# Forward convolution in a hand-set order, and the down-gradient stores on another DMA queue

## The chip, the cores and the metric

One core of one Trainium2 chip. The metric is the device time of one execution in microseconds, the median of 13 runs: 2044.87 us before (2031.46 to 2072.03).

## What is computed

Forward and backward of a gated block on S = 2048 rows, D = 1024 channels, F = 3584 hidden columns, all in bf16:

```python
x = A_q; xn = layernorm(x)
k_shift = sum(k_pad[:, t:t+S] * shift_k[:, ks-1-t] for t in range(4))   # causal, 4 taps
kv = k_shift * v
y = irfft(rfft(kv, 2S) * rfft(ssm_k, 2S))[:S] + kv * ssm_D              # long convolution per channel
s = xn * y
b = ((xn @ w_up) * (xn @ w_gate)) @ w_down
out = x + s * silu(b)
```

The outputs are `out` and the gradients of nine inputs (q, k, v, the shift and convolution weights, D, and the three matrices), for a given `grad_out`.

## The kernel before

The kernel runs in five stages, each bound to a long stream of matmuls on TensorE; the vector work of the convolutions runs beside them. TensorE, VectorE (DVE), ScalarE (ACT), GpSimd (POOL) and SyncE (SP) each run their own instructions in order. SP, ACT and POOL each start DMAs on a queue of their own: `ld` is SP's (L60), `st` POOL's (L65), `sta` ACT's (L71). The order on an engine is chosen by a scheduler from the order of the program and from dependencies; `tc.issue_after(x)` holds an instruction back until after `x` in that order, and `tc.keep_in_program_order` (under `PIN[0]` for VectorE, L205) pins it to where the program has it.

1. Gate and up (L585; to about 577 us). 28 slabs of 256 columns, each against 16 row blocks. A group is 8 matmuls into one psum tile; ScalarE copies it to `gut` (L587), two buffers; four groups are a unit (`gu_unit`). A unit ends with the product gate x up on VectorE into `hN` (L591), its store to `Hd`, and, five groups later, its turn: 8 transposes on TensorE and a store to `HTd`. The first two slabs run block by block behind the layer norm of each chunk of rows. From slab 2 on `tick` is called after each group and pumps the generator `conv_forward` on: the generator yields a weight for each piece of work, in us of VectorE, and the pump takes pieces until their sum has the share of the total that the count of groups has.
2. Down product and the gate's derivative (L988; 577 to 768 us).
3. Gradient of h, and of w_up and w_gate (L1119 and L1136; to 1395 us).
4. Gradient of w_down (L1244, the down gradient; 1395 to 1633 us). For each of 14 slabs of h: a load of 1 MB on SP, two slabs ahead, into three buffers (`load_h`, L1151); 4 groups of 16 matmuls into one of four `psb` buffers; a copy on ScalarE into `wbs` (four buffers, L1246); and two stores of 256 KB on ACT's queue (L1249). Between the loads SP issues DMA transposes of w_gate and w_up (L1202, 1 MB each) and of the gradient dgu (L1209) for the next stage. `tc.issue_after(h_ld[0].ins)` (L1217) puts them after the slab's load. The backward convolution's last units run beside it on VectorE; POOL loads 1 MB tiles A and B for them and stores their results, and slab 11 drains them (L1224) and frees their memory for more transposes.
5. Gradient of x (L1267; from 1633 us to the end), with the dk part beside it.

The forward convolution handles 128 channels at a time, in eight groups `ds`. The steps of one: for each pair of groups the 4-tap shift on VectorE, two halves of 1024 rows (`shift`, L630), ending in `kv`; the filter's rows turned on TensorE (`h_rows`, L651); for kv and then for the filter a forward transform (`fwd4`, L235): four pieces of 16 matmuls (`psF`), each copied to `SP` by ScalarE, then eight additions on VectorE through `W` into `KX` or `HX`; two additions to turn HX (L677); the product of the two on VectorE (`product`, L317); the inverse's additions into `HX` (`inv_dft`, L351); and at last 32 matmuls `psY` with four copies and a store (`tail`, L684). `staggered` (L466) runs one group's tail 12 us of weight into the next group's main part. VectorE's instructions of this stage aren't pinned.

Of the kernel before, what the change touches and what calls it, by code (L numbers as in the profile page):

```python
# [13 lines left out]
BF16 = mybir.dt.bfloat16  # L14
# [5 lines left out]
def build_kernel(  # L20
# [213 lines left out]

    def fwd4(x, X, wp, psp, first=None):  # L235

        W = wp.tile([P, 2, 2, 4, 256], F32, name="W", tag="W")
        c, d = W[:, 0], W[:, 1]
        for i in range(2):
            SP = wp.tile([P, 2, 2, 512], F32, name="SP", bufs=2)  # L240
            for par in range(2):
                ps = psp.tile([P, 2, 2, 256], F32, name="psF")
                cmm(ps[:, 0], T4[par], x, (i, i + 4), first if i == 0 else None)
                cmm(ps[:, 1], T4[par], x, (i + 2, i + 6))
                nc.scalar.copy(out=SP[:, :, par], in_=ps[:].rearrange("p s k x -> p s (k x)"))  # L245
                yield 0.1
            s, q = [SP[:, j].rearrange("p a (k x) -> p (a k) x", k=2) for j in range(2)]
            tt(c[:, i], s, q, ADD)
            tt(d[:, i], s, q, SUB)
            yield 2.5  # L250
        tt(X[:, 0:4, :], c[:, 0], c[:, 1], ADD)
        tt(X[:, 8:12, :], c[:, 0], c[:, 1], SUB)
        yield 2.5
        d0, d1 = [d[:, i].rearrange("p (a k) x -> p a k x", a=2) for i in range(2)]
        tt(two(X, 4, 2, 9), d0, d1[:, :, ::-1], ADD)
        tt(two(X, 12, 2, -7), d0, d1[:, :, ::-1], SUB)
        yield 2.5
    FWD4_W = 0.4 + 4 * 2.5

# [257 lines left out]
    def layer_norm(b0, n, x4):  # L517
# [44 lines left out]
        return last, root, st(xnn[:, c, r0:r0 + n, :], x4[:, 0:n, :])  # L562

    later = []
    gu_mm = [None]
# [4 lines left out]
    def flush(age=0):  # L570
# [3 lines left out]
        while later and later[0][0] >= age:  # L574
            later.pop(0)[1]()

    def gu_unit(sl, b0, n, w, tick):

        gut = fg.tile([P, 2, 4, SLW], BF16, name="gut")
        hN = fg.tile([P, 4, SLW], BF16, name="hN", bufs=3)  # L580
        for i in range(n):
            q, qi = divmod(b0 + i, 4)
            ps = ps_gu.tile([P, 512], F32, name="psg")
            for dc in range(DC):
                gu_mm[0] = nc.tensor.matmul(ps[:], XNT[q][:, dc, qi * P:(qi + 1) * P],  # L585
                                            w[:, dc].rearrange("p a f -> p (a f)"), start=(dc == 0), stop=(dc == DC - 1))
            nc.scalar.copy(out=gut[:, :, i], in_=ps[:].rearrange("p (a f) -> p a f", a=2))  # L587
            flush(5)
            tick()
        sta(GUd[sl, b0 // 8][:, :, b0 % 8:b0 % 8 + n], gut[:, :, 0:n])  # L590
        tt(hN[:, 0:n], gut[:, 0, 0:n], gut[:, 1, 0:n], MUL)  # L591
        st(Hd[sl][:, b0:b0 + n, :], hN[:, 0:n])

        def turn():
            hT = fg.tile([P, 2, 4, P], BF16, name="hT")
            ps = ps_tr.tile([P, 2, 4, P], BF16, name="tr")
            for a in range(2):
                for i in range(n):
                    nc.tensor.transpose(ps[:, a, i, :], hN[:, i, a * P:(a + 1) * P], ident[:])
            nc.scalar.copy(out=hT[:, :, 0:n], in_=ps[:, :, 0:n])  # L600
            fr, so = sl % 12 * SLW, b0 % 8 * P
            st(HTd[b0 // 8][sl // 12][fr:fr + SLW, so:so + n * P].rearrange("(a f) s -> f a s", f=P),
               hT[:, :, 0:n].rearrange("f a i s -> f a (i s)"))
        defer(turn)

    h_out = []

    def conv_forward():
# [21 lines left out]
        def shift(dp):  # L630
# [3 lines left out]
            for c in range(2):  # L634
                k, v = S_.pop(("kv", dp, c))
                acc = U[7][:, 0:2048].rearrange("p (e r d) -> p e r d", e=2, r=8)
                with tc.issue_after(last.ins):
# [13 lines left out]
        def h_rows(ds):  # L651
            hrow = S_.pop(("h", ds))
            hx = cs.tile([P, NB, P], BF16, name="hx")
            for c in range(2):
# [5 lines left out]
                nc.scalar.activation(hx[:, 8 * c:8 * c + 8, :], ps[:], ACT.Copy, scale=WSC)  # L660
                yield 0.1
            h_out.append(ds)
# [3 lines left out]

        def main(ds):
            if ds % 2 == 0:
                yield from shift(ds // 2)
            kvs = S_["kvt", ds // 2][:, ds % 2]  # L670
            yield from h_rows(ds)
            KX = cx.tile([P, 16, 256], BF16, name="KX")
            yield from fwd4(kvs, KX, cs, ps_cv)
            st(KFd[ds], KX[:])
            HX = cs.tile([P, 16, 256], BF16, name="HX", bufs=2)
            yield from fwd4(S_["hx"], HX, cs, ps_cv, S_.pop(("D", ds))[:])
            turned(HX, 1, 0, 1)  # L677
            yield 1.4
            st(HFd[ds], HX[:])
            yield from product(KX, HX, KX, cs, False, 0)  # L680
            yield from inv_dft(KX, HX, cs)
            S_["G", ds] = HX

        def tail(ds):  # L684
            G = S_.pop(("G", ds))
            yf = cs.tile([P, NB, P], BF16, name="yf")
            for rp in range(4):
                ps = inv_rows(G, ps_y, rp)
                nc.scalar.copy(out=by_res(yf[:], rp), in_=rowps(ps))
                yield 0.1  # L690
            st(YFd[:, :, ds * P:(ds + 1) * P], yf[:])

        load_h(0)
        load_kv(0, 0)
        load_kv(0, 1)
        tl = None
        for ds in range(8):
            yield from staggered(main(ds), tl, 12.0)
            tl = tail(ds)
        yield from tl  # L700
        kst.release()
        cs.release()
        cx.release()

    F_TOTAL = 4 * 20.0 + 8 * (0.2 + 2 * FWD4_W + 1.4 + PROD_W + INV_W + 0.4)
    nop = lambda: None
    chunks = [(0, 1), (1, 1), (2, 2), (4, 4), (8, 4), (12, 4)]
# [20 lines left out]
    for i, (b0, n, x4) in enumerate(xs):  # L728
        if i + 1 < len(xs):
            with tc.issue_after(last.ins):  # L730
                last, root, xst = layer_norm(*xs[i + 1])
        for sl in range(2):
            gu_unit(sl, b0, n, slabs[sl], nop)
            if i in (3, 4):
                with tc.issue_after(gu_mm[0].ins):
                    for j in ((3,), (2,), (1,), (0,))[2 * (i - 3) + sl]:
                        bcast(j)
        if i == len(xs) - 1:
# [13 lines left out]
    def tick():  # L752
        cnt[0] += 1
        pump(cnt[0] / NT)

    for sl in range(2, NSL - 2):
        w, wld = load_slab(sl, nc.sync)
# [24 lines left out]
    for hf in range(2):  # L782
        if hf == 1:
            flush()
            load_wd(2)
            wd_ld = load_wd(3)
            ld(HT0[1][:, 8:12], ht_rows(0, 24, 28))
        for sl in range(NSL - 2, NSL):
            for b0 in (8 * hf, 8 * hf + 4):
                gu_unit(sl, b0, 4, slabs[sl - NSL + 2], tick)  # L790
            if (hf, sl) == (0, NSL - 2):

                assert len(h_out) == 8
                ld(HT0[1][:, 0:8], ht_rows(0, 16, 24))
    flush()
    drain()
    for p_ in (ps_cv, ps_y, ps_tr, ps_gu, fg, fw):
        p_.release()
# [349 lines left out]

    h_ld = [None]

    def load_h(sl):  # L1151
        h = u8(HSL[sl % 3], "p (b f) -> p b f", b=NB)
        h_ld[0] = ld(h, Hd[sl])
        hs[sl] = h
# [59 lines left out]
    for k in range(NSL):  # L1214
        if k + 2 < NSL:
            load_h(k + 2)
        with tc.issue_after(h_ld[0].ins):  # L1217
            if k in (1, 2, 3, 4, 5):
# [20 lines left out]
        for f in range(2):  # L1239
# [8 lines left out]
            f0 = k * SLW + f * P  # L1248
            sta(o_dwd[f0:f0 + P, :], wbs)  # L1249
    for p_ in (ps_y4[0], ps_b, wo):  # L1250
# [144 lines left out]
```

## Time and profile before

| | us |
|---|---|
| median of 13 runs | 2044.87 |
| profiled execution | 2050.49 |
| its span, first to last instruction | 2048.7 |
| TensorE busy | 1964.1 (96%) |
| VectorE busy | 1433.8 (70%) |
| ScalarE busy | 648.1 (32%) |
| GpSimd busy | 344.2 (17%) |
| mean granted TensorE clock | 0.985 |

A row of a timeline has the start, the duration, the engine, the line, the operation, what it writes <- what it reads, and in brackets the idle time of its engine before it and what ended that. PEld is TensorE's weight load, beside the matmuls. An SPq or ACTq row is the issue of a DMA: its duration is how long the queue's engine was held by it, not the transfer. A row of waits names who waited <- for whom, the sum in us, how often, and the longest. A DMA transpose moves packets of 256 bytes, a load of 1 MB packets of 8 KB. Line numbers are those of the kernel before; most VectorE operations go through one helper and stand at L206.

### The profile page before, as it was taken

The page shows a single profiled execution, that of the slowest core. Times are in us where ns is not written, and L with a number is a line of the kernel's source. Part 1 is how long each engine was busy: PE and PEld are TensorE (multiplying, and loading weights), DVE is VectorE, ACT ScalarE, POOL GpSimd, SP SyncE. Part 2 cuts the span into 40 slices and gives each one's busy share as a digit, 9 for nine tenths or more (in the row PEclk, how much of TensorE's full clock was granted, in tenths as well). Part 3 has the DMA queues.
Part 4 walks back from the last instruction along what each step waited for, and adds up shares of the span by engine and source line. Part 5 has one row for each costly group of instructions (what it writes and reads, how often), then busy time and mean ns, then how long its engine had stood idle before and what let it go on. Part 6 is the DMA issues. An engine that isn't in the chain of part 4 may idle for free.

```text
span 2048.7 us, 27740 instructions
## 1 busy us (share of the span) xinstructions
PE 1964.1 (96%) x11288; PEld 1053.3 (51%) x11288; DVE 1433.8 (70%) x1576; ACT 648.1 (32%) x954; POOL 344.2 (17%) x496
## 2 busy tenths in 40 slices
PE   6999999999999999999999999999969799999998
PEld 3455555545544446665566656654434344444443
DVE  7779898978836556886999899999845024444343
ACT  4755554546432224432222222221112101111112
POOL 3322222111112211001021212112102000110100
PEclk9999999999999999999999999999989999999999
DMA  9686666557699987656686996666997989393931
GB/s 300 229 283 221 202 216 209 201 185 244 229 289 292 292 281 263 224 188 212 244 262 233 248 264 212 245 229 202 144 208 185 184 191 219 108 214 97 208 92 57
DMA packets 422529, 440.74 MB, mean 215 GB/s; under 512 B 248961, under 2 KB 336825, under 8 KB 408577
## 3 DMA queue, kind: packets, MB, share of 16 engines
q1 hardware_dynamic: 329472, 211.06, 40.9%
q0 software_dynamic: 42112, 176.51, 26.9%
q10 hardware_dynamic: 50816, 51.39, 7.9%
q8 instruction: 88, 1.44, 0.3%
q14 instruction: 41, 0.33, 0.1%
HBM read 198.72 MB, written 189.83 MB: 190 GB/s over the span
## 4 chain that ended last, share of the span: by engine, by line
PE 60%; issue 17%; DVE 9%; SPq 5%; POOL 4%; DMA 2%; ACT 1%; POOLq 0%; ACTq 0%; DVEq 0%
PE psx L1267 18%; PE psb L1136 18%; PE psb L1119 8%; PE psb L1244 5%; PE psg L585 5%; SPq L1202 4%; DVE W L206 2%; DVE HX L206 2%; PE psF L230 2%; SPq L1209 1%; DVE m L206 1%; DVE KX L206 1%; PE psdk L964 1%; PE psY L420 1%; POOL HTd L66 1%
## 5 line engine op out<-in xcount | busy, mean ns | idle before, releaser
L585 PE MATMUL psg<-wslab,U 128*128 128x512 bf16 x1792 | 414.7, 384 | 7.8 <-ACT U L558 5.3
L1136 PE MATMUL psb<-U,U 128*128 128x512 bf16 x1792 | 396.8, 379 | 0.0
L1267 PE MATMUL psx<-U,dgut 128*128 128x512 bf16 x1536 | 335.7, 379 | 1.7 <-ACT wbs L1246 1.7
L1267 PEld LDWEIGHTS <-dgut 128*128 128x128 bf16 x1792 | 174.0, 98 | 212.6 <-issue 5.4
L1136 PEld LDWEIGHTS <-U 128*128 128x128 bf16 x1792 | 175.4, 98 | 198.9 <-issue 0.3
L585 PEld LDWEIGHTS <-U 128*128 128x128 bf16 x1792 | 174.7, 99 | 200.1 <-issue 12.5
L1244 PE MATMUL psb<-U,U 128*128 128x512 bf16 x896 | 199.3, 385 | 30.2 <-DMA U<-Hd 20.9
L1119 PE MATMUL psb<-wdt,U 128*128 128x256 bf16 x1792 | 206.4, 273 | 1.1 <-DMA U<-XNd 1.1
L587 ACT CAST gut<-psg 128x512 bf16<-128x512 f32 x224 | 131.4, 587 | 200.4 <-PE psg L585 188.2
L1119 PEld LDWEIGHTS <-U 128*128 128x128 bf16 x1792 | 175.5, 98 | 31.5 <-issue 1.4
L988 PE MATMUL psbm<-U,ht 128*128 128x512 bf16 x784 | 169.9, 379 | 0.0
L1141 ACT CAST wb<-psb 128x512 bf16<-128x512 f32 x112 | 65.6, 586 | 312.0 <-PE psb L1136 309.2
L1244 PEld LDWEIGHTS <-U 128*128 128x128 bf16 x896 | 88.3, 99 | 138.8 <-DMA U<-Hd 21.4
L206 DVE TENSOR_TENSOR W<-W 128x1024 f32<-128x1024 f32 (+1 forms) x144 | 149.7, 1057 | 3.0
L206 DVE TENSOR_TENSOR W<-SP 128x1024 f32<-128x1024 f32 x96 | 112.4, 1220 | 43.8 <-ACT SP L245 34.0
L206 DVE TENSOR_TENSOR dka<-dkh,Wbc 128x1024 bf16<-128x1024 bf16 x16 | 11.1, 692 | 187.1 <-DMA dkh<-DKSHd 187.1
L1290 ACT ACTIVATE dx_t<-dxn 128x1024 bf16<-128x1024 f32 (+1 forms) x17 | 17.1, 1007 | 342.2 <-DVE dxn L206 288.1
L988 PEld LDWEIGHTS <-ht 128*128 128x128 bf16 x784 | 76.6, 98 | 91.8
L206 DVE TENSOR_TENSOR m<-A,B 128x2048 bf16<-128x2048 bf16 (+1 forms) x48 | 73.4, 1576 | 47.1 <-issue 28.2
L1121 ACT CAST dht<-psb 128x512 bf16<-128x512 f32 x112 | 65.7, 586 | 116.8 <-PE psb L1119 106.3
L206 DVE TENSOR_TENSOR U<-U,dht 128x2048 bf16<-128x2048 bf16 x56 | 71.1, 1270 | 44.4 <-ACT dht L1121 44.3
L1246 ACT CAST wbs<-psb 128x512 bf16<-128x512 f32 x56 | 32.4, 587 | 196.8 <-PE psb L1244 153.3
(203 smaller groups left out, 2283.3 us busy)
## 6 DMA issues: line engine op xcount, KB each, us to landing
U<-GUd SPq DMA_DIRECT2D x28, 1024.0 KB, 8.4
DGd<-U SPq DMA_DIRECT2D x28, 1024.0 KB, 4.7
GUd<-gut ACTq DMA_DIRECT2D x54, 512.0 KB, 4.4
A<-DYFd POOLq DMA_DIRECT2D x16, 1024.0 KB, 9.6
out_dram<-wb ACTq DMA_DIRECT2D x112, 128.0 KB, 5.4
U<-Hd SPq DMA_DIRECT2D x14, 1024.0 KB, 7.0
Hd<-hN POOLq DMA_DIRECT2D x54, 256.0 KB, 4.2
HTd<-hT POOLq DMA_DIRECT2D x54, 256.0 KB, 4.0
```

The costliest lines, as they stand in the source:

```text
L206: ins = V.tensor_tensor(o, a, b, op)
L230: nc.tensor.matmul(ps[:, k].rearrange("p (c d) -> p c d", c=2), T[:, r, k, :], xr[:, r], start=(n == 0), stop=(n == len(rs) - 1 and (first ...
L585: gu_mm[0] = nc.tensor.matmul(ps[:], XNT[q][:, dc, qi * P:(qi + 1) * P], w[:, dc].rearrange("p a f -> p (a f)"), start=(dc == 0), stop=(dc ...
L587: nc.scalar.copy(out=gut[:, :, i], in_=ps[:].rearrange("p (a f) -> p a f", a=2))
L988: nc.tensor.matmul(ps[:, dh * 512:(dh + 1) * 512], ht(fc)[:, i * P:(i + 1) * P], WD[fc // 4][:, fc % 4, dh * 512:(dh + 1) * 512], start=(f ...
L1119: nc.tensor.matmul(ps[:, x * SLW:(x + 1) * SLW], DBMT[2 * hf + g][:, dc, (b % 4) * P:(b % 4 + 1) * P], wdt[:, dc, :], start=(dc == 0), sto ...
L1121: nc.scalar.copy(out=dht[:, 2 * e:2 * e + 2].rearrange("p b f -> p (b f)"), in_=ps[:])
L1136: nc.tensor.matmul(ps[:], XN[b // 4][:, b % 4, dc * P:(dc + 1) * P], dgus[b // 8][:, :, b % 8], start=(b == 0), stop=(b == NB - 1))
L1141: nc.scalar.copy(out=wb[:, dc % 2].rearrange("p a f -> p (a f)"), in_=ps[:])
L1202: nc.sync.dma_start_transpose(out=store, in_=(B_w_gate, B_w_up)[a][:, j * 512:(j + 1) * 512])
L1244: nc.tensor.matmul(ps[:], h[:, b, f * P:(f + 1) * P], DBM[b // 4][:, b % 4, dh * 512:(dh + 1) * 512], start=(b == 0), stop=(b == NB - 1))
L1267: nc.tensor.matmul(ps[:, dh * 512:(dh + 1) * 512], t[n][:, f, i * P:(i + 1) * P], WGU[n][:, f, dh * 512:(dh + 1) * 512], start=(n == 0 and ...
```

## The change

In stage 1, `fwd4` is split into the transform's matmuls and copies of one half (`fwd4_half`), the sums of a half, and the two output steps. `conv_forward` becomes one loop that sets these steps one by one: the next group's two kv halves are put between the steps of this group's inverse (`ahead`), the first half of the filter's transform before the outputs of kv's, and the four `psY` pieces between the steps of the next group. VectorE's instructions are pinned to the program's order from there to the stage's end. The shift's accumulator alternates between two buffers (`U[7 - c]`). The product gate x up of a unit is held (`hn`) until the first group of the next unit is copied. The last chunks of the first two slabs run in another order: slab 0 with chunk 5 before slab 1 with chunk 4. The pump is run to a weight of 20 before slab 2, and the weights are set anew.

In stage 4, the two stores per slab go to SP's queue (`ld` for `sta`), and the transposes are put after the last store of the slab before, not after the slab's load.

```diff
...
 
-    def fwd4(x, X, wp, psp, first=None):
+    def fwd4_half(x, i, wp, psp, first=None):
 
-        W = wp.tile([P, 2, 2, 4, 256], F32, name="W", tag="W")
+        SP = wp.tile([P, 2, 2, 512], F32, name="SP", bufs=2)
+        for par in range(2):
+            ps = psp.tile([P, 2, 2, 256], F32, name="psF")
+            cmm(ps[:, 0], T4[par], x, (i, i + 4), first if i == 0 else None)
+            cmm(ps[:, 1], T4[par], x, (i + 2, i + 6))
+            nc.scalar.copy(out=SP[:, :, par], in_=ps[:].rearrange("p s k x -> p s (k x)"))
+        return SP
+
+    def fwd4_buf(wp):
+        return wp.tile([P, 2, 2, 4, 256], F32, name="W", tag="W")
+
+    def fwd4_sums(W, SP, i):
+        s, q = [SP[:, j].rearrange("p a (k x) -> p (a k) x", k=2) for j in range(2)]
+        tt(W[:, 0, i], s, q, ADD)
+        tt(W[:, 1, i], s, q, SUB)
+
+    def fwd4_outs(X, W, n):
         c, d = W[:, 0], W[:, 1]
-        for i in range(2):
-            SP = wp.tile([P, 2, 2, 512], F32, name="SP", bufs=2)
-            for par in range(2):
-                ps = psp.tile([P, 2, 2, 256], F32, name="psF")
-                cmm(ps[:, 0], T4[par], x, (i, i + 4), first if i == 0 else None)
-                cmm(ps[:, 1], T4[par], x, (i + 2, i + 6))
-                nc.scalar.copy(out=SP[:, :, par], in_=ps[:].rearrange("p s k x -> p s (k x)"))
-                yield 0.1
-            s, q = [SP[:, j].rearrange("p a (k x) -> p (a k) x", k=2) for j in range(2)]
-            tt(c[:, i], s, q, ADD)
-            tt(d[:, i], s, q, SUB)
-            yield 2.5
-        tt(X[:, 0:4, :], c[:, 0], c[:, 1], ADD)
-        tt(X[:, 8:12, :], c[:, 0], c[:, 1], SUB)
-        yield 2.5
-        d0, d1 = [d[:, i].rearrange("p (a k) x -> p a k x", a=2) for i in range(2)]
-        tt(two(X, 4, 2, 9), d0, d1[:, :, ::-1], ADD)
-        tt(two(X, 12, 2, -7), d0, d1[:, :, ::-1], SUB)
-        yield 2.5
-    FWD4_W = 0.4 + 4 * 2.5
+        if n == 0:
+            tt(X[:, 0:4, :], c[:, 0], c[:, 1], ADD)
+            tt(X[:, 8:12, :], c[:, 0], c[:, 1], SUB)
+        else:
+            d0, d1 = [d[:, i].rearrange("p (a k) x -> p a k x", a=2) for i in range(2)]
+            tt(two(X, 4, 2, 9), d0, d1[:, :, ::-1], ADD)
+            tt(two(X, 12, 2, -7), d0, d1[:, :, ::-1], SUB)
+    FWD4_W = 8 * 2.4
 
...
 
+    nop = lambda: None
     later = []
...
 
+    hn = [nop]
+
     def gu_unit(sl, b0, n, w, tick):
...
             flush(5)
+            hn[0]()
+            hn[0] = nop
             tick()
         sta(GUd[sl, b0 // 8][:, :, b0 % 8:b0 % 8 + n], gut[:, :, 0:n])
-        tt(hN[:, 0:n], gut[:, 0, 0:n], gut[:, 1, 0:n], MUL)
-        st(Hd[sl][:, b0:b0 + n, :], hN[:, 0:n])
+
+        def multiply():
+            tt(hN[:, 0:n], gut[:, 0, 0:n], gut[:, 1, 0:n], MUL)
+            st(Hd[sl][:, b0:b0 + n, :], hN[:, 0:n])
+            defer(turn)
+        hn[0] = multiply
 
...
                hT[:, :, 0:n].rearrange("f a i s -> f a (i s)"))
-        defer(turn)
 
...
                 k, v = S_.pop(("kv", dp, c))
-                acc = U[7][:, 0:2048].rearrange("p (e r d) -> p e r d", e=2, r=8)
+                acc = U[7 - c][:, 0:2048].rearrange("p (e r d) -> p e r d", e=2, r=8)
                 with tc.issue_after(last.ins):
...
                 nc.scalar.activation(hx[:, 8 * c:8 * c + 8, :], ps[:], ACT.Copy, scale=WSC)
-                yield 0.1
             h_out.append(ds)
...
 
-        def main(ds):
-            if ds % 2 == 0:
-                yield from shift(ds // 2)
-            kvs = S_["kvt", ds // 2][:, ds % 2]
-            yield from h_rows(ds)
-            KX = cx.tile([P, 16, 256], BF16, name="KX")
-            yield from fwd4(kvs, KX, cs, ps_cv)
-            st(KFd[ds], KX[:])
-            HX = cs.tile([P, 16, 256], BF16, name="HX", bufs=2)
-            yield from fwd4(S_["hx"], HX, cs, ps_cv, S_.pop(("D", ds))[:])
-            turned(HX, 1, 0, 1)
-            yield 1.4
-            st(HFd[ds], HX[:])
-            yield from product(KX, HX, KX, cs, False, 0)
-            yield from inv_dft(KX, HX, cs)
-            S_["G", ds] = HX
+        def kvs(ds):
+            return S_["kvt", ds // 2][:, ds % 2]
 
...
                 nc.scalar.copy(out=by_res(yf[:], rp), in_=rowps(ps))
-                yield 0.1
-            st(YFd[:, :, ds * P:(ds + 1) * P], yf[:])
+                if rp == 3:
+                    st(YFd[:, :, ds * P:(ds + 1) * P], yf[:])
+                yield
 
...
         load_kv(0, 1)
-        tl = None
+        yield from shift(0)
+        PIN[0] = True
+        yield 6.0
+        h_rows(0)
+        tl = iter(())
+        sp = [fwd4_half(kvs(0), i, cs, ps_cv) for i in range(2)]
         for ds in range(8):
-            yield from staggered(main(ds), tl, 12.0)
+            yield 0.5
+            W = fwd4_buf(cs)
+            fwd4_sums(W, sp[0], 0)
+            yield 2.4
+            fwd4_sums(W, sp[1], 1)
+            D0 = S_.pop(("D", ds))[:]
+            sph = [fwd4_half(S_["hx"], 0, cs, ps_cv, D0)]
+            yield 2.4
+            KX = cx.tile([P, 16, 256], BF16, name="KX")
+            fwd4_outs(KX, W, 0)
+            sph.append(fwd4_half(S_["hx"], 1, cs, ps_cv, D0))
+            yield 2.4
+            fwd4_outs(KX, W, 1)
+            st(KFd[ds], KX[:])
+            next(tl, None)
+            yield 2.4
+            W = fwd4_buf(cs)
+            for i in range(2):
+                fwd4_sums(W, sph[i], i)
+                next(tl, None)
+                yield 2.4
+            if ds < 7:
+                h_rows(ds + 1)
+            HX = cs.tile([P, 16, 256], BF16, name="HX", bufs=2)
+            for i in range(2):
+                fwd4_outs(HX, W, i)
+                next(tl, None)
+                yield 2.4
+            turned(HX, 1, 0, 1)
+            yield 1.3
+            st(HFd[ds], HX[:])
+            yield from product(KX, HX, KX, cs, False, 0)
+            if ds % 2 == 1 and ds < 7:
+                yield from shift(ds // 2 + 1)
+            sp = []
+
+            def ahead():
+                if ds < 7:
+                    sp.append(fwd4_half(kvs(ds + 1), len(sp), cs, ps_cv))
+            yield from inv_dft(KX, HX, cs, ahead, ahead)
+            S_["G", ds] = HX
             tl = tail(ds)
-        yield from tl
+        yield 6.0
+        for _ in tl:
+            yield 1.0
         kst.release()
...
 
-    F_TOTAL = 4 * 20.0 + 8 * (0.2 + 2 * FWD4_W + 1.4 + PROD_W + INV_W + 0.4)
-    nop = lambda: None
+    F_TOTAL = 4 * 20.0 + 6.0 + 8 * (0.5 + FWD4_W + 1.3 + PROD_W + INV_W) + 10.0
     chunks = [(0, 1), (1, 1), (2, 2), (4, 4), (8, 4), (12, 4)]
...
                 last, root, xst = layer_norm(*xs[i + 1])
-        for sl in range(2):
-            gu_unit(sl, b0, n, slabs[sl], nop)
-            if i in (3, 4):
+        for i_, sl in ([(i, 0), (i, 1)] if i < 4 else ([(4, 0)], [(5, 0), (4, 1), (5, 1)])[i - 4]):
+            gu_unit(sl, *xs[i_][0:2], slabs[sl], nop)
+            if i_ in (3, 4):
                 with tc.issue_after(gu_mm[0].ins):
-                    for j in ((3,), (2,), (1,), (0,))[2 * (i - 3) + sl]:
-                        bcast(j)
+                    bcast((3, 2, 1, 0)[2 * (i_ - 3) + sl])
         if i == len(xs) - 1:
...
         cnt[0] += 1
-        pump(cnt[0] / NT)
+        pump((20.0 + (F_TOTAL - 20.0) * cnt[0] / NT) / F_TOTAL)
 
+    pump(20.0 / F_TOTAL)
     for sl in range(2, NSL - 2):
...
         if hf == 1:
+            hn[0]()
+            hn[0] = nop
             flush()
...
                 ld(HT0[1][:, 0:8], ht_rows(0, 16, 24))
+    hn[0]()
     flush()
     drain()
+    PIN[0] = False
     for p_ in (ps_cv, ps_y, ps_tr, ps_gu, fg, fw):
...
 
-    h_ld = [None]
-
     def load_h(sl):
         h = u8(HSL[sl % 3], "p (b f) -> p b f", b=NB)
-        h_ld[0] = ld(h, Hd[sl])
+        ld(h, Hd[sl])
         hs[sl] = h
...
             load_h(k + 2)
-        with tc.issue_after(h_ld[0].ins):
+        with tc.issue_after(wst.ins) if k > 0 else nullcontext():
             if k in (1, 2, 3, 4, 5):
...
             f0 = k * SLW + f * P
-            sta(o_dwd[f0:f0 + P, :], wbs)
+            wst = ld(o_dwd[f0:f0 + P, :], wbs)
     for p_ in (ps_y4[0], ps_b, wo):
```

## The prediction

> **What bounds the kernel now.** I read the page's engine table, then TensorE's waits, then the timelines around the largest of them.
>
> ```profile
> PE 1964.1 (96%) x11288; PEld 1053.3 (51%) x11288; DVE 1433.8 (70%) x1576; ACT 648.1 (32%) x954; POOL 344.2 (17%) x496
> ```
>
> TensorE sets the time: 96% busy, some 85 us idle. Only idle time (and the slow clock after it) can be won; the change adds and removes no matmul. TensorE's waits over the whole span:
>
> ```profile
> PE psb L1244 <- DMA U<-Hd: 20.9, 1, 20.9
> PE psY L431 <- DVE HX L206: 13.9, 5, 4.4
> PE psb L1244 <- ACT wbs L1246: 9.3, 3, 6.1
> ...
> PE psx L1267 <- ACT wbs L1246: 1.7, 1, 1.7
> ```
>
> The second row is the forward convolution; the others are the down-gradient stage. The rest of the idle time (start, tail, small waits) is not touched. First the convolution, one row of TensorE's timeline, one of VectorE's:
>
> ```profile
> 221.84 0.97 PE L431 MATMUL psY<-HX,TI 128*128 128x256 bf16 x4 [3.94 <-DVE HX L206]
> ...
> 235.45 2.36 DVE L206 TENSOR_TENSOR W<-SP 128x1024 f32<-128x1024 f32 x2 [6.89 <-ACT SP L245]
> ```
>
> The two engines wait for each other in turn: TensorE reaches a channel group's last rows before VectorE has HX, and 13 us later VectorE has nothing, because the next group's transform stands behind those rows on TensorE. The windows, around the convolution and for four stretches with DMA transposes (columns: window, length, busy PE, PEld, DVE, ACT, POOL, granted clock, DMA share, GB/s):
>
> ```profile
> 71.00:556.00 485.00, 468.33 (x2899) 262.25 (x2899) 430.85 (x383) 261.75 (x367) 110.12 (x169) 0.98 0.67 225
> ...
> 1455.00:1497.00 42.00, 26.66 (x124) 11.91 (x122) 36.97 (x35) 4.69 (x8) 1.85 (x4) 0.86 1.18 144
> ...
> 1583.00:1602.00 19.00, 16.23 (x76) 7.22 (x74) 0.00 (x0) 0.59 (x1) 0.00 (x0) 1.00 1.03 55
> ...
> 1650.00:1671.00 21.00, 21.00 (x103) 9.43 (x101) 4.76 (x7) 0.00 (x0) 1.96 (x3) 1.00 1.15 229
> 1690.00:1721.00 31.00, 31.00 (x167) 14.45 (x166) 13.24 (x17) 3.77 (x6) 3.71 (x7) 1.00 1.11 213
> ```
>
> All four stretches have DMA shares above 1, but 55 and 144 GB/s moved where SP's transposes, POOL's loads and ACT's stores run together, 229 and 213 where only SP's transposes and POOL's loads do. SP's queue shows what that does:
>
> ```profile
> 1409.42 7.93 SPq L1202 DMA_TRANSPOSE U<-in_B_w_gate_dram  x1
> 1424.65 0.33 SPq L61 DMA_DIRECT2D U<-Hd  x1
> 1425.03 27.52 SPq L1202 DMA_TRANSPOSE U<-in_B_w_up_dram  x1
> 1452.64 0.53 SPq L61 DMA_DIRECT2D U<-Hd  x1
> 1453.22 40.59 SPq L1202 DMA_TRANSPOSE U<-in_B_w_gate_dram  x1
> 1493.91 0.73 SPq L61 DMA_DIRECT2D U<-Hd  x1
> ```
>
> One transpose holds SP for 7.9, 27.5 or 40.6 us; the H load behind the longest leaves at 1493.91 and TensorE stands from 1481.7 to 1502.6. At the stage's end ScalarE's own queue stands:
>
> ```profile
> 1585.45 0.59 ACT L1246 CAST wbs<-psb 128x512 bf16<-128x512 f32 x1 [2.87 <-PE psb L1244]
> 1604.21 0.34 ACTq L72 DMA_DIRECT2D out_dram<-wbs  x1
> 1604.64 1.07 ACT L1246 CAST wbs<-psb 128x512 bf16<-128x512 f32 x2 [18.60 <-DMA dgut<-DGd]
> ```
>
> The copy is done at 1586.0, its store leaves only at 1604.21, behind a transpose's completion: SP's and ACT's DMAs take turns on shared completion semaphores (the built order shows the store waiting for such a one). The next copies queue behind it and TensorE's four psb buffers fill.
>
> **The convolution, part by part.** VectorE's work stays the same; its order changes. From the first shift product at 71.2 to the last HX at 556.2 the trace has 455.7 us of VectorE instructions in 485, so 29.3 idle. TensorE idles 16.7 us there and 2 us after it (0.8 and 1.1). Each psY stall over 3.9 us is followed by half clock: 3.4, 6.8 and 6.8 us granted at 0.5, so 17.1 x 0.5 = 8.5 us. TensorE's whole stake is 16.7 + 2 + 8.5 = 27 us.
>
> In the built order of the changed kernel the next group's two kv halves and its first h half stand before the psY rows of the group before (kv at the 79th, h at the 82nd, psY from the 84th gate/up group; before, psY at 83 to 86 and kv from 86). The mutual wait goes. What is late next is VectorE itself: per pair of channel groups it has 2 x 42 (transforms, product) + 16 x 1.22 (shift) + 11.5 x 0.68 (hN) = 111 us, TensorE 46 x 1.73 + 11.5 x 0.43 + 2 x 11.4 = 107. So VectorE cannot be far ahead: without any idle it ends at 71.2 + 455.7 = 527, TensorE without stalls near 531. Every us of VectorE idle beyond 4 is paid. I take 10 us of idle for the program order now pinned: HX ends at 537, a gain of 19, less 2 for a remaining half-clock window: **17 us** (bounds: 27 if all goes; a loss of 10 if the pinned order makes VectorE idle 40).
>
> The side edits: the multiply is held until the next unit's first group, so a pinned VectorE doesn't wait 1.73 us or more for a copy; its H store on POOL and its turn move with it, one group, with POOL 17% busy: nothing. If VectorE lags more than a unit (some 8 us), the two gut buffers fill and TensorE waits; that is the 10 us of loss above. The second accumulator removes VectorE's 6.9 us wait for the KSHd store, inside the 29.3. Chunk 5's slab-0 unit before chunk 4's slab-1 unit frees the slab four groups earlier: its 1.95 us wait is in the 16.7.
>
> **The down-gradient stage.** 28 stores of 256 KB leave ScalarE (28 x 0.34 = 9.5 us of issue) for SP (28 x 0.4 = 11 us, on an engine that is only a queue). No engine instruction changes. On SP each store waits for its copy; behind it stand the H loads and the next transposes, and TensorE waits for those. The H load needs the same slab's end that the second store waits for, so it loses nothing but 0.4 us; the first store is due at mid-slab, 6.9 us earlier. A load has 27.6 us (two slabs of 13.8) before its use.
>
> - ScalarE no longer waits for SP's completions: the 6.05, 1.74, 1.55 and 1.66 us at the stage's end, 11.0 us, and 6.8 us of half clock from 1604.3, of which TensorE ran 5.8: 2.9. Sum 14.
> - The 20.9 us: it goes if the second and third transposes take 8 to 15 us. There is then no ACT queue in the stage. The nearest rows are the two of 1650 and 1690: the same queues, 229 and 213 GB/s. There the POOL loads are 352 KB, here 1 MB, so I stretch: 160 packets of POOL there cost the transposes some 5 us, 1 MB then 10. Then 20.9 + 2.8 x 0.5 = 22 go; if not, 0; if the stores behind the transposes add a stall, minus 20.
>
> A rule speaks against this. The Trainium skill, "DMA: Bandwidth & Descriptors", section "Issuing engines are not separate DMA queues", has all queues share the same 16 DMA engines and interleave, so a second issuing engine only saves issue time; the same page asks nothing of a transpose next to ordinary DMAs. By the rule the transposes stay at 27 and 41 us and the stage wins only the 14 us of ScalarE's waits. By the rows a third queue costs a factor of 1.5 to 4 in moved bytes, and the stage wins 14 + 22 = 36. I follow the rows, since every slow transpose of this stage with a stall behind it lies in a three-queue stretch.
>
> What is late next: SP's own transposes. They run without a gap from 1571.6 to 1671.1, and the last piece is needed 13 x 3.47 us into the dx stage, at about 1680, some 5 us after it lands. If dx starts 36 us earlier, the transposes must too. Their start waits for the backward convolution's end, which follows TensorE and moves by the 22; the 16 us standstill in 1584 to 1602 is worth another 11; the six stores between them cost 4.5. So 36 can be taken less some 3: **33 us**.
>
> **Sum.** The profiled execution took 2050.5 us (span 2048.7): 2050.5 - 17 - 33 = 2000.5. It lies 5.6 above the median of 13, and the 13 scatter over 40 us, as they would if collisions of queues differ in length; a kernel without them ends at the same floor from either, so I take the sum itself: **2000 us**.
>
> **Rivals.**
> - Both gains, 0.56: 2000; own range 1986 to 2016.
> - POOL's megabyte loads alone slow the transposes. For it: at 1434 to 1435, with no ACT packet under way, they had already slowed. Against it: 1650 to 1721. Stage wins 11: 2050.5 - 17 - 11 = 2022. 0.17.
> - The pinned VectorE order gives back what it wins, as 111 over 107 allows; the stage still wins: 2050.5 - 33 = 2017. 0.07. With the rival above: 2040. 0.05.
> - Slower, 0.15: SP becomes the stage's bottleneck. Four wbs buffers of 6.9 us cover 27.6 us; once one transpose holds SP longer, stores and H loads queue behind it together, ScalarE's copy waits for a buffer, and TensorE stops at each collision. With the 20.9 kept, two more stalls of that size and 17 won: 2050.5 + 42 - 17 = 2075. It decides from a transpose of 28 us; two in the trace are at it or past it.
>
> Differences under 0.3% (6 us) cannot be told from none. Faster 0.56 + 0.17 + 0.07 = 0.80, same 0.05, slower 0.15. The range takes in all but the slower case and a little of the first: 1986 to 2042.
>
> **What would show it.** Right: TensorE's waits have no U<-Hd row and no wbs row above 2 us, no L1202 transpose lasts over 15 us, the stage moves over 200 GB/s where loads meet transposes, psY waits sum under 5 us, VectorE idles under 12 us in the convolution. Wrong: transposes still of 25 us or more without ACT stores (second rival), "wbs <- DMA out_dram" on ScalarE (the slower case), psg waiting for gut copies in the first 550 us (third), or psx waiting for WGU or dgut, which would mean that the gain was handed on to the dx stage.

## The result, and the profile after

The changed kernel takes 2016.6 us (median of 11 runs, 2011.4 to 2023.5); the kernel before, beside it, 2046.0 (median of 48, 2031.5 to 2072.0). The ratio is 0.9866, 95% interval 0.9839 to 0.9892: faster by 1.3%, some 27 us (29 by the medians). The ratio leaves out the executions of the kernel before that fell in a slower state of the chip, so it is nearer to 1 than the quotient of the medians. The scatter fell too, from 41 us to 12. The forecast was 2000 with a range of 1986 to 2042: the sign was right, 16.6 us of the gain did not come, and steps behind it were wrong.

Line numbers are now those of the changed kernel; the psb copies of the down-gradient stage stand at L1292 and its transposes at L1248 and L1255. The profiled execution took 2019.26 us (2050.49 before). TensorE's share of the span, then its waits above 4 us, and from the same view those of the down-gradient stage and the entry of the dx stage:

```profile
PE 1961.8 (97%) x11288; PEld 1052.6 (52%) x11288; DVE 1441.6 (71%) x1576; ACT 648.5 (32%) x954; POOL 344.2 (17%) x496
```

```profile
PE tr L560 <- DVE x L557: 8.6, 2, 7.7
PE psF L230 <- DVE kv L206: 6.4, 4, 2.2
PE psx L1313 <- ACT wbs L1292: 4.8, 1, 4.8
PE psx L1313 <- DVE dxn L206: 4.7, 1, 4.7
PE psg L592 <- ACT U L562: 4.2, 2, 3.0
...
PE psb L1290 <- DMA U<-Hd: 0.7, 1, 0.7
PE psx L1313 <- DMA U<-in_B_w_up_dram: 0.6, 1, 0.6
```

The three rows that the forecast wanted gone are gone (psY <- HX 13.9, psb <- U 20.9, psb <- wbs 9.3). Three smaller ones are new: psF <- kv in the convolution, psx <- wbs at the entry of the dx stage, psx <- dxn inside it.

Cutting both traces at the first matmul of each stage gives where the 31.2 us between the two profiled executions went:

| stage | before | after | difference | forecast |
|---|---|---|---|---|
| gate/up with convolution, from the start | 573.6 | 563.4 | -10.2 | -17 |
| down product | 196.0 | 196.0 | 0 | 0 |
| gradients of h, w_up, w_gate | 625.4 | 626.4 | +1.0 | 0 |
| down gradient | 239.9 | 208.8 | -31.1 | -36 |
| dx | 413.7 | 422.8 | +9.1 | +3 |

The convolution's window over the stretch shown before, then four in the down-gradient stage (columns as there: window, length, busy PE, PEld, DVE, ACT, POOL, granted clock, DMA share, GB/s):

```profile
71.00:556.00 485.00, 476.58 (x2961) 267.17 (x2960) 435.57 (x384) 267.16 (x376) 113.14 (x174) 0.99 0.69 228
1416.00:1434.00 18.00, 18.00 (x85) 8.16 (x84) 17.69 (x19) 3.00 (x6) 0.53 (x1) 1.00 1.09 218
1450.00:1482.00 32.00, 32.00 (x174) 15.51 (x172) 31.45 (x30) 4.11 (x7) 0.53 (x1) 1.00 1.18 145
...
1546.00:1552.00 6.00, 6.00 (x30) 2.70 (x29) 0.00 (x0) 1.17 (x2) 2.36 (x4) 1.00 1.13 246
1553.00:1566.00 13.00, 13.00 (x62) 5.88 (x61) 0.00 (x0) 2.34 (x4) 0.00 (x0) 1.00 1.12 54
```

TensorE is now busy in 476.6 of the 485 us, against 468.3. The row at 1450 is the one that contradicts the forecast: ACT's queue carries nothing in this stage any more, and still only 145 GB/s move at a DMA share of 1.18. The queues in that stretch (q1 carries SP's DMAs, q0 POOL's; ACT's q10 has no packet; then packets, MB, share of the 16 engines), and SP's own rows:

```profile
q1 hardware_dynamic: 4171, 2.52, 86.4%
q0 software_dynamic: 312, 2.13, 31.2%
```

```profile
1416.47 16.96 SPq L1248 DMA_TRANSPOSE U<-in_B_w_up_dram  x1
1433.52 1.54 SPq L61 DMA_DIRECT2D out_dram<-wbs  x1
...
1436.24 11.15 SPq L1248 DMA_TRANSPOSE U<-in_B_w_gate_dram  x1
...
1450.25 30.73 SPq L1248 DMA_TRANSPOSE U<-in_B_w_up_dram  x1
1481.08 0.53 SPq L61 DMA_DIRECT2D out_dram<-wbs  x1
1481.70 0.38 SPq L61 DMA_DIRECT2D U<-Hd  x1
```

Two transposes of the same megabyte still take 17 and 31 us (27.5 and 40.6 before), but a third of 11 us now stands between them. ScalarE and TensorE show how near the longest came to costing time:

```profile
1472.52 0.59 ACT L1292 CAST wbs<-psb 128x512 bf16<-128x512 f32 x1 [2.82 <-PE psb L1290]
1484.92 0.59 ACT L1292 CAST wbs<-psb 128x512 bf16<-128x512 f32 x1 [11.82 <-DMA out_dram<-wbs]
1488.81 7.51 PE L1290 MATMUL psb<-U,U 128*128 128x512 bf16 x34 [0.73 <-DMA U<-Hd]
```

The four wbs buffers ran out at 1473 and ScalarE stood for 11.8 us; the four psb buffers behind it (4 x 3.46 us of matmuls) took that up. The 0.7 us that TensorE lost is the H load: it stood behind the transpose, left at 1481.70 and landed at 1488.77, just after TensorE wanted it.

### The profile page after: what moved, and what is told of

Its sections match the earlier page's. It is cut to its first block, busy times and chain, and to the rows that moved or that the text cites. A ratio compares the mean times of both kernels' runs of the same rounds, so it can differ in the third digit from the quotient of the medians.

```text
span 2017.5 us, 27727 instructions
## 1 busy us (share of the span) xinstructions
PE 1961.8 (97%) x11288; PEld 1052.6 (52%) x11288; DVE 1441.6 (71%) x1576; ACT 648.5 (32%) x954; POOL 344.2 (17%) x496
## 5 line engine op out<-in xcount | busy, mean ns | idle before, releaser
L206 DVE TENSOR_TENSOR dka<-dkh,Wbc 128x1024 bf16<-128x1024 bf16 x16 | 11.1, 692 | 182.6 <-DMA dkh<-DKSHd 182.6
L1336 ACT ACTIVATE dx_t<-dxn 128x1024 bf16<-128x1024 f32 (+1 forms) x17 | 17.1, 1007 | 347.8 <-DVE dxn L206 239.3
L1292 ACT CAST wbs<-psb 128x512 bf16<-128x512 f32 x56 | 32.6, 587 | 165.6 <-PE psb L1290 121.1
```

What stands on the lines that cost most here:

```text
L206: ins = V.tensor_tensor(o, a, b, op)
L1292: nc.scalar.copy(out=wbs[:, dh * 512:(dh + 1) * 512], in_=ps[:])
```

## The experiments

Each ran beside the kernel before, from whose time its ratio is taken; "profiled" is its profiled execution. Two theories were at stake. Mine, after the result: POOL's 1 MB loads beside SP's transposes are what slows them; ACT's stores only pass the delay on. The rival is the forecast's own step: the third queue is what costs bandwidth.

**One part alone.** The convolution's edits with the old stage 4, and the old convolution with the new stage 4:

```diff
 e1_conv_only (changed kernel)
-        with tc.issue_after(wst.ins) if k > 0 else nullcontext():
+        with tc.issue_after(h_ld[0].ins):
...
-            wst = ld(o_dwd[f0:f0 + P, :], wbs)
+            sta(o_dwd[f0:f0 + P, :], wbs)
 e2_stores_only (kernel before): the same lines the other way
```

> The convolution's new order alone; the down-gradient stage as before. The changed kernel's trace puts the convolution's gain at 10 us (psY waits gone, 6.4 us of new psF waits). If the two parts are independent: 2046 - 10 = 2036, and the 20.9 us wait for an H load in some form is still there, with transposes of 25 to 41 us. Rival, the stage's stall is a matter of when transposes meet POOL's loads, and a shift of the stage by 10 us is enough to remove it: 2015.

> The stage's change alone; the convolution as before. Independent parts: 2046 - 31 + 9 (given back in the dx stage) = 2024 to 2028, no U<-Hd wait above 2 us. Rival, the two parts need each other: within 6 us of before.

Measured: e1 2032.9 us, ratio 0.9923 (0.9883 to 0.9963); e2 2032.1, 0.9896 (0.9833 to 0.9959). Of the kernel before's time that is some 16 us (8 to 24) and 21 us (8 to 34), together 37; the two at once give 27, which is within these intervals. Profiled, the gate/up stage of e1 is 8.7 us shorter than before; the down-gradient stage of e2 is 211.7 us against 239.9. e1 shows something more: its stage 4 is the old code, its transposes take 20.6 and 28.3 us, and no U <- Hd wait appears; the stage takes 218.9. Its first two transposes and POOL's loads leave at the same distance from the stage's start as in the kernel before, within 1.2 us. So 21 of the 31 us in the table above were a stall that this one execution of the kernel before had and another, with the same stage 4, had not. What stays in e1 is the wait through ACT:

```profile
1575.92 0.34 ACTq L72 DMA_DIRECT2D out_dram<-wbs  x1
1576.36 1.07 ACT L1294 CAST wbs<-psb 128x512 bf16<-128x512 f32 x2 [20.69 <-DMA dgut<-DGd]
1587.28 0.34 ACTq L72 DMA_DIRECT2D out_dram<-wbs  x1
1587.72 1.07 ACT L1294 CAST wbs<-psb 128x512 bf16<-128x512 f32 x2 [10.29 <-DMA dgut<-DGd]
```

ACT's stores wait for completions of SP's transposes, as the forecast read it. In this program SP's and ACT's DMAs count on the same eight semaphores: the store of 1575.92 waits for the one of a dgut transpose that SP issued at 1552.82 and that landed at 1575.85. TensorE's psb <- wbs wait is 11.1 us here.

**The queue or the place.** Stage 4's two edits apart: stores on SP with the transposes still behind the H load, and stores on ACT with the transposes meant to stand behind the last store.

```diff
 e3_queue_only (changed kernel)
-        with tc.issue_after(wst.ins) if k > 0 else nullcontext():
+        with tc.issue_after(h_ld[0].ins):
 e4_place_only (changed kernel)
-            wst = ld(o_dwd[f0:f0 + P, :], wbs)
+            wst = sta(o_dwd[f0:f0 + P, :], wbs)
```

> The changed kernel with the transposes again behind the slab's load and not behind the last store; the stores stay on SP. If the queue is what counts (no third queue, no waits of ScalarE for SP's completions): 2015 to 2020 as the changed kernel. If the turn counts (a transpose behind the stores meets POOL's loads less): 2030 or more with a U<-Hd wait of 10 to 20 us.

> The changed kernel with the stores on ScalarE's queue again; the transposes stay behind the last store of the slab before. If the queue counts: the wbs waits of 11 us and the U<-Hd wait come back, 2036 to 2046. If the turn counts: 2016 to 2025.

Measured: e3 2019.8 us, 0.9847 (0.9786 to 0.9907), within the noise of the changed kernel; e4 2031.1, 0.9898 (0.983 to 0.9966). By e3 the queue alone gives what the change gives, as far as these runs can tell. e4 is not the test that it was meant to be: `issue_after` named a store of ACT's, and that did not hold SP back. The five transposes of the weights and the first eight of dgut left between 1382 and 1433 us, the first ahead of the stage's first matmul (1384.6):

```profile
1382.21 5.05 SPq L1248 DMA_TRANSPOSE U<-in_B_w_gate_dram  x1
...
1415.12 17.97 SPq L1255 DMA_TRANSPOSE dgut<-DGd  x8
```

None of the five takes over 9.1 us, and TensorE has no wait for U <- Hd; still psb <- wbs keeps 6.8 us (profiled, stage 4 is 216.1 against 212.8 in e3). The place alone was not tried, and the intervals of e3 and e4 overlap.

**POOL's loads or the third queue.** The last A and B loads of the backward convolution go from POOL to SP, in the changed kernel and in the kernel before, where ACT's stores stay.

```diff
 e5_one_queue (changed kernel), e8_loads_sp_before (kernel before)
-                cld(As[n][:], DYFd[units[n][1]])
+                (ld if n >= 10 else cld)(As[n][:], DYFd[units[n][1]])
...
-                cld(Bs[n][:], units[n][2][units[n][1]])
+                (ld if n >= 10 else cld)(Bs[n][:], units[n][2][units[n][1]])
```

> The changed kernel with the 1 MB loads A and B of the backward convolution's last six units on SP, in turn with the transposes, so that no POOL load meets a transpose before the drain. If POOL's loads are what slows transposes: no L1248 transpose of 1 MB above 12 us up to the drain (17, 11 and 31 us in the changed kernel). Time: 2016 within 6, as the changed kernel has hardly a stall left there, or slower by the waits of SP for VectorE. If ACT's stores were the cause, the transposes stay as in the changed kernel.

> The kernel before with only the loads A and B of the last six units on SP; the stores stay on ScalarE's queue. If POOL's loads alone slow the transposes: 27 and 41 us fall under 12, the U<-Hd wait of 20.9 us goes, the ScalarE waits of 11 us stay: 2046 - 22 = 2024. If ACT's stores beside transposes are what slows them: they stay above 20 us and the time within 6 us of before.

Measured: e5 2020.0 us, 0.9853 (0.9776 to 0.9929), like the changed kernel; e8 2036.1, 0.9942 (0.9903 to 0.998), some 12 us (4 to 20) less than its kernel before, with a scatter of 14 us. SP's queue and two windows of e8, where SP's and ACT's queues run and POOL's has no packet:

```profile
1429.71 0.32 SPq L61 DMA_DIRECT2D A<-DYFd  x1
1430.13 0.38 SPq L61 DMA_DIRECT2D B<-KFd  x1
1430.60 0.38 SPq L61 DMA_DIRECT2D U<-Hd  x1
1431.04 12.40 SPq L1202 DMA_TRANSPOSE U<-in_B_w_up_dram  x1
...
1466.78 11.26 SPq L1202 DMA_TRANSPOSE U<-in_B_w_up_dram  x1
```

```profile
1431.00:1444.00 13.00, 13.00 (x62) 5.93 (x61) 9.94 (x11) 2.34 (x4) 0.00 (x0) 1.00 1.06 322
1466.00:1478.00 12.00, 12.00 (x57) 5.46 (x56) 10.72 (x12) 1.75 (x3) 0.00 (x0) 1.00 0.99 338
```

The slow pair of transposes takes 12.4 and 11.3 us with ACT's stores in place, and 322 to 338 GB/s move at a DMA share of 1.06 and 0.99. e5 has 12.2 and 10.7. That settles it against the third queue: with ACT's stores and without POOL's loads the transposes are fast; without the stores and with POOL's loads (the changed kernel) they are slow. Why SP's loads do no harm, e8's packets tell, from 1431 to 1438 and from 1440 to 1444:

```profile
DMA packets 410, 2.59 MB, mean 370 GB/s; under 512 B 31, under 2 KB 31, under 8 KB 116
DMA packets 3074, 0.81 MB, mean 203 GB/s; under 512 B 3070, under 2 KB 3070, under 8 KB 3071
```

In the first stretch the loads run, and a store of ACT's, in the second the transpose (packets of 256 bytes): the 12.4 us that the transpose holds SP are for the most part time behind three loads, and the two meet for some 2 us at most. With the loads on POOL both are under way together for 22 us (1458 to 1480 in the changed kernel), the transpose's packets take 162 ns on average (26 in e8's second stretch), and 67 GB/s move. So what is shown is that the meeting slows both. Whether it must be POOL's queue is open: these loads were not tried on ACT's.

TensorE's psb <- wbs wait stays at 11.4 us in e8: the coupling through ACT is a second, separate cost, and of the edits tried only moving the stores takes it out of the stage. In e5 the fast transposes bring no time, because hardly anything waited for the transposes any more.

**The convolution's order.** Three runs of the changed kernel: VectorE not pinned; the next pair's shift ahead of the product, so that kv is there earlier; and the unit's multiply not held.

```diff
 e6_no_pin
-        PIN[0] = True
 e7_shift_early
+            if ds % 2 == 1 and ds < 7:
+                yield from shift(ds // 2 + 1)
             yield from product(KX, HX, KX, cs, False, 0)
-            if ds % 2 == 1 and ds < 7:
-                yield from shift(ds // 2 + 1)
 e11_no_hold
-        hn[0] = multiply
...
+        multiply()
```

> The changed kernel without pinning VectorE's order in the convolution; the scheduler places it. If the new loop's order alone wins the 10 us: 2016 within 4. If the pin is needed: 2020 to 2028, with psY or psF waits of 10 us or more in the first 560 us.

> The changed kernel with the next pair's shift ahead of the product and not between product and inverse. The psF waits for kv (6.4 us, three of 2 us and their half clock) should go: 2016 - 6 - 3 = 2007 to 2012. If VectorE's total work is the bound and not the place of the shift, the wait turns up at psY with the same sum: 2016 within 3.

> The changed kernel with the hN multiply at the end of its own gate/up unit instead of being held until the next unit's first group; the order of VectorE stays pinned. My prediction's statement: a pinned VectorE then waits for the unit's last copy, 1.7 us or more for each of some 92 units in the convolution stretch, and as VectorE and TensorE are about equally loaded there (VectorE 455.8 us busy of 468.5) what it loses beyond some 10 us is paid: HX(7) ends 30 us or more later than 535.9 and the time is 2040 to 2080. Rival (TensorE is ahead of VectorE there, so the copy is long done when VectorE comes to the multiply): hold worth nothing, time 2012 to 2022, HX(7) within 3 us of 535.9.

Measured: e6 2021.6 us, 0.9861 (0.9785 to 0.9937); e7 2014.2, 0.9817 (0.9724 to 0.9911); e11 2018.0, 0.9888 (0.9852 to 0.9923). None can be told from the changed kernel. My statement on the hold falls: without it HX is done at 536.6 us instead of 535.9 and nothing is lost. VectorE waits 20.9 us for gut copies there and 21.3 with the hold. In e7 the psF <- kv wait becomes another one:

```profile
PE psF L230 <- ACT SP L242: 6.6, 3, 2.9
```

The stage ends at 563.5 us in e7 and 563.4 in the changed kernel: the wait moved from VectorE's product to ScalarE's copy, its length stayed.

**Is the next standstill also POOL's load?** At 1554.4 us five dgut transposes hold SP for 24.4 us in the changed kernel, beside POOL's loads of kh and dkh. Here these two go to SP.

```diff
 e9_kh_sp (changed kernel)
-            cld_k(kh[:], c, ds)
+            q = ld if i == 0 else cld
+            ksrc = KSLd[ds]
+            q(kh[:], bass.AP(ksrc.tensor, ksrc.offset + 1024 * c * P, [[8 * P, P], [P, 11], [1, P]]))
...
-            cld(dk[:], bass.AP(src.tensor, src.offset + 1024 * c * P, [[8 * P, P], [P, 11], [1, P]]))
+            q(dk[:], bass.AP(src.tensor, src.offset + 1024 * c * P, [[8 * P, P], [P, 11], [1, P]]))
```

> The changed kernel, with the first pair of kh and dkh loads of the kernel-gradient step (352 KB each, the ones that POOL issued at 1547.3 and 1547.8 in the changed kernel's profile) on SP's queue instead. Theory (a load that POOL issues is what slows SP's transposes): the row of five dgut transposes beside them falls from 24.4 us to some 8 to 10, the 4.8 us wait of psx for wbs at the entry of dx goes, since the stores behind it on SP leave earlier, and the time falls by 3 to 8 us against the changed kernel's 2016.6. Rival (the 24.4 us are the work of the transposes themselves or of the DGd rows that they read): the row stays at 20 us or more and the time stays within 3 us. Since kh and dkh now stand among the transposes in SP's queue, psdk may wait for them by some us; that would show as a row psdk <- dkh.

Measured: 2033.7 us, 0.9951 (0.9917 to 0.9985), 17 us slower than the changed kernel. The theory fell and the edit had a price of its own. SP's queue and TensorE's wait in e9:

```profile
1552.34 21.25 SPq L1257 DMA_TRANSPOSE dgut<-DGd  x5
...
1605.76 0.42 SPq L61 DMA_DIRECT2D dkh<-DKSHd  x1
```

```profile
1609.29 1.28 PE L1014 MATMUL psdk<-kh,dkh 128*64 128x256 bf16 x10 [22.04 <-DMA dkh<-DKSHd]
```

No load of POOL is near, and the row still takes 21.3 us. dkh now stands behind a queue of transposes and leaves SP at 1605.76; TensorE, which has it next, stands for 22 us. What starts at 1551 is told by the windows of e9 and by POOL's queue:

```profile
1543.00:1550.00 7.00, 7.00 (x35) 3.17 (x33) 0.00 (x0) 1.20 (x3) 1.90 (x3) 1.00 1.16 255
1551.00:1563.00 12.00, 12.00 (x57) 5.45 (x56) 0.00 (x0) 1.76 (x3) 0.00 (x0) 1.00 1.00 54
```

```profile
1543.76 0.54 POOL L66 DMA_DIRECT2D out_dram<-ho  x1 [0.30 <-POOL ho L979]
1544.29 0.91 POOL L66 DMA_DIRECT2D out_dram<-ddo  x1
```

The last store of POOL there is `ddo`, the gradient of D: 1024 values of 2 bytes, each to its own address from 128 partitions by 8 columns. Its 16 packets of 128 bytes (the only ones of that size on POOL's queue there) start between 1550.7 and 1551.0, and all DMA traffic falls from 255 to 54 GB/s with the engines counted busy. In every one of the 14 profiles, those of before (1583.6 us) and after (1552.8) included, the traffic is 236 to 265 GB/s in the 8 us up to these packets, 5 to 41 in the 9 us that begin 1 us after them, and back 10 to 19 us after them. The stretch of 55 GB/s that the forecast put down to three queues is this one; in the changed kernel, with no packet on ACT's queue, it has 54. The longest waits of ScalarE for dgut, in before, e1, e4 and e8 (17.8 to 20.7 us), fall into it too. That is a coincidence in time, seen 14 times, and not an experiment: a kernel without that store, or with its values gathered into one row first, was not tried, and the first dgut transposes that follow the load of W stand at the same place in all 14.

**Put together.**

```diff
 e12_early_one_queue: e7 and e5
 e10_best: e7, e5 and e9
```

> The changed kernel with the two edits that each helped a little or nothing alone: the shift of the next pair ahead of the product, and the A and B loads of the backward convolution's last units on SP in turn with the transposes. Theory: the parts lie in different stages and add: 2014.2 by the first, 2020.0 by the second (changed kernel 2016.6), so 2012 to 2020, no more than 4 us below the changed kernel. Rival (the stages are coupled through SP's queue and the H loads): over 2022 or below 2008.

> All three together: the shift ahead of the product, the A and B loads and the first kh and dkh loads on SP. No transpose of the down-gradient stage then stands beside a load that POOL issues. Theory: no transpose over 13 us in that stage and no dgut row over 12 us, no wait of TensorE for U or wbs over 2 us, stage of 206 to 210 us, dx stage 415 to 420, time 2005 to 2014. Rival (what stays is VectorE's and TensorE's own load): the rows are short but the time is 2012 to 2020 like the changed kernel's.

Measured: e12 2016.9 us, 0.9869 (0.9818 to 0.9919); e10 2030.4, 0.9946 (0.9916 to 0.9976). e12 has fast transposes and the early shift and is no faster than the change alone; e10 has e9's wait (24.1 us for dkh) and its price. No version beats the changed kernel by more than the noise.

## Why the prediction was right, and where it was wrong

The profiled sum was 2000.5 and the profiled execution came at 2019.3. The 18.8 us between are 6.8 in the convolution, 4.9 in the down-gradient stage, 6.1 more handed on to dx, and 1.0 between.

- **Convolution, mechanism right, size wrong: 17 forecast, 10.2 measured.** HX was done at 535.9 us (forecast 537) and the psY waits are gone. The failed step is the one from there to "a gain of 19": it took HX's end for the stage's. HX's end moved by 20.3 us, the stage's by 10.2, and what follows HX grew from 17.4 to 27.5 us. e6 says the same: HX is done at 529.4 there, and the stage ends at 563.4 as in the changed kernel. TensorE ends the stage, and its idle time in it fell by 8.7 us (36.4 to 27.7). The term behind that is "TensorE's whole stake is 16.7 + 2 + 8.5", of which all but a little was to be had. Two things lessen it. Half clock counted at 17.1 x 0.5 overlaps the stalls: some 4 us of the 17.1 lay inside idle time already counted, so its loss was 6.5; and 6.8 us of half clock stay. And a new wait of 6.4 us, psF <- kv, came from the very order that removed the old one; I had allowed 2 us for what would remain. e7 did not get these back: its wait moved to ScalarE's copy, 6.6 us. That no order could is not shown.

  The count of VectorE was off as well: 455.7 us are durations added up, and records that overlap count twice; the forecast's own window has 430.85 busy, so VectorE idled 54 us of 485, not 29.3. In the changed kernel it idles 33 of 468 (12.7 by the forecast's count, where 10 were forecast), 21 of them behind the gut copies that follow TensorE, so "every us of VectorE idle beyond 4 is paid" did not hold.

  And 10.2 is one pair of profiles: the stage takes 573.5 to 582.2 us in the three with the old convolution and 562.4 to 565.5 in the six with the new one as it is.
- **The stores' wait for SP's completions: right, less a part that moved.** e1, e4 and e8, all with stores on ACT, keep 11.1, 6.8 and 11.4 us of psb <- wbs; e3 and the change, with the stores on SP, have none in the stage. At the entry of dx 4.8 us stand (psx <- wbs, 1.7 before), which the 14 had as won: of 11.0 us of waits for wbs 6.2 went.
- **"By the rows a third queue costs a factor of 1.5 to 4 in moved bytes": wrong.** The changed kernel moves 145 GB/s without ACT's queue, e8 322 with it and without POOL's loads. Of the two slow stretches that I compared, one was POOL's 1 MB loads and the other, by all signs, the 2-byte store. The comparison with 229 and 213 GB/s changed the number of queues and the size of the loads together, and I charged it to the first. The rival "POOL's megabyte loads alone slow the transposes" had the mechanism, but not the time: it left the 20.9 us stall standing, and it went. So the 22 of the 36 came without their cause, and that the stage's sum came near (31.1) is luck.

  Of the five signs that were to show the forecast right only the psY waits came: transposes of 17 and 31 us, 145 GB/s, 4.8 us of psx <- wbs and VectorE's idle time were misses. Two signs of being wrong came, a transpose over 25 us without ACT's stores and ScalarE's wait for `out_dram`.
- **The rule that spoke against the change.** "DMA: Bandwidth & Descriptors" in the Trainium skill, section "Issuing engines are not separate DMA queues", was right that taking the stores off ACT frees no bandwidth: 144 GB/s in the slow stretch before, 145 after. It also says that DMAs of different engines interleave. What it doesn't say, and this case shows, is what that can cost: the transposes take 17 and 31 us where POOL's A and B loads interleave with them, and 12.2 and 10.7 where the same loads stand ahead of them in SP's queue (e5). The page's other sentence, on a transpose next to ordinary DMAs, stands in its section "Rules for kernel authors", on which DMAs have to wait for one another, and is no statement on speed.
- **The 20.9 us: a draw.** e1 has the same stage 4 and doesn't show it. The forecast took it as a feature of the kernel, since it stood in the profiled execution; the wide scatter of the runs (41 us) was the hint that it varied. e1, with the same stage, scatters over 34 us, e8, without POOL's loads beside the transposes, over 14. A second profile of the kernel before would settle it; there is none. The median gained nearly as much as the profile all the same (29.4 against 31.2 us).
- **Handed on to dx: 3 forecast, 9.1 measured.** New there are 4.7 us of psx <- dxn, 0.6 of psx <- U, and half clock of which some 3.7 count (4.0 us of it after the entry's stall, 3.4 after the other, each at half). One row of VectorE's timeline in the changed kernel shows where the 4.7 come from:

```profile
1800.64 0.69 DVE L206 TENSOR_TENSOR dka<-dkh,Wbc 128x1024 bf16<-128x1024 bf16 x1 [17.68 <-DMA dkh<-DKSHd]
...
1805.48 1.22 DVE L206 TENSOR_TENSOR dxn<-psx,dxna_t 128x1024 f32<-128x1024 f32 x1
```

  VectorE waits 17.7 us for a dkh load, and the addition that frees TensorE's psx stands behind it.
- **The slower case** set the point at one transpose of 28 us. There was one of 30.7, and TensorE lost 0.7: I had counted the wbs buffers and left out the four psb buffers behind them, 13.8 us more. But the H load behind that transpose landed with nothing to spare, so a longer one would have cost TensorE all the same: the case was missed by about a microsecond.

## What to carry to other kernels

When two stretches of a profile differ in speed, list everything that differs between them, down to the smallest store, before giving the difference to one of them; then move only that one. See too, in the trace, that the move does what it should: e4's did not. A stall of one profiled execution is a sample, and a wide scatter of the runs says so. A load moved to another queue leaves when everything ahead of it there has left: e9's 352 KB cost 22 us of TensorE because they stood behind transposes.

## What the hardware showed

- A 1 MB DMA transpose holds SP for 5.7 to 7.9 us as the first of the stage (13 profiles, e4 aside), the two beside POOL's 1 MB loads for 17 to 41 us (nine profiles), and for 10.5 to 12.4 us where SP issues those loads ahead of it (e5, e8, e10, e12).
- A store of 1024 single 2-byte values (2 KB) is followed in every profile by a standstill of 10 to 19 us, in whose first part the 16 DMA engines count as busy and move 5 to 41 GB/s; cause by timing only.
- Of three TensorE stalls of about 2 us (psF <- kv) two were followed by 3.4 us of half clock; the two of 4.75 us went with 6.8 and 3.4 (changed kernel).
